# One attention-plus-mixer kernel: the mixer at six products a pair, and part of the output products moved between the row maxima

## The chip, the cores and the metric

The kernel runs on one core of a Trainium2 chip. The metric is the device time of one execution in microseconds (us); less is better.

## The reference

The input `x` has 2048 tokens of 512 channels. Two branches read its layernorm `xn`: a softmax attention with 32 heads of 16 channels, and the token-mixing block of MLP-Mixer, whose two matrices act along the tokens. The second branch gates the first.

```python
def _A_ref(x, wqkv, wo):                       # H = 32, Dh = 16
    qkv = (x @ wqkv).reshape(B, S, 3, H, Dh).transpose(2, 0, 3, 1, 4)
    q, k, v = qkv[0], qkv[1], qkv[2]
    p = softmax(einsum("bhqd,bhkd->bhqk", q, k) * Dh ** -0.5)
    o = einsum("bhqk,bhkd->bhqd", p, v)
    return o.transpose(0, 2, 1, 3).reshape(B, S, D) @ wo
def _B_ref(x, w1, b1, w2, b2):                 # F = 1792
    h = layernorm(x)
    u = gelu(einsum("bsd,sf->bdf", h, w1) + b1)
    return (einsum("bdf,fs->bds", u, w2) + b2).transpose(0, 2, 1)
xn = layernorm(x)
out = x + _A_ref(xn, A_wqkv, A_wo) * silu(_B_ref(xn, B_w1, B_b1, B_w2, B_b2))
```

All data are float32. Where the kernel multiplies matrices of the mixer or the output, each factor is held as an upper and a lower part in TensorE's one-pass format, and three products (upper by upper, upper by lower, lower by upper) are added.

## The kernel before, in words

**Stages.** A first stage of some 150 us makes q, k and v and stores them in DRAM. Then one hand-written loop over `s` (0 to 532 by two) does all the rest; one turn of it is called a *pair* here. Heads are worked two at a time: 16 head pairs `p`, each with two *spans* of 1024 queries and 16 blocks of keys. In one pair TensorE (PE) makes

- eight *maxima products* (`max_of`, L386) of queries by keys, 512 columns each, of which VectorE (DVE) takes row maxima (L390), while `s` is below `NU` = 512;
- eight *scores* (`score`, L724) with the maximum already subtracted through two extra rows of the operands; ScalarE (ACT) exponentiates them (L729) into `prob`;
- two times the *values* (`values`, L740): four 32-column products of `prob` by v and ones, summed over the 16 key blocks in the bank `av`.

Scores run 20 steps (`LEAD`) behind the maxima, so the loop has three parts: ten pairs with maxima alone, 246 *steady pairs* (`s` = 20 to 510) with both, and a *tail* of ten pairs (`s` = 512 to 530) with scores and values but without maxima. A closing stretch behind it finishes the last head pair (`own`, `one`, `two`, `chunk`) and writes the last eight row blocks.

**The filler.** All other work of PE is a list of *products* of 512 columns that a generator `everything()` gives out (`mixer()`, then `rest()`). In a steady pair `halves` takes up to six of them, cuts each into two pieces of 64 rows (L864), and `ORDERS` lays the pieces (D) between maxima (m) and scores (s) of the two heads:

```python
    2: ("smsmDDsmsm", "msmsmsmsDD", 3),
    4: ("sDDDDmsmsmsm", "msmsmsmDDDDs", 6),
    6: ("DDDDDDsmsmsmsm", "msmsmsmsDDDDDD", 7),
```

The first word is that of one head, the second that of the other, read position by position; at the number the values come in. How many are taken is set by `wanted(s)`, a straight line from the products done at the start to `n_fill` = 1344 at the pair `T_MIX`. Outside the steady pairs `whole` makes a product in one piece of 128 rows (L839).

**The mixer** has 14 blocks of 48 products (layer 1) and 16 blocks of 42 (layer 2), 1344 in all. A block sums in the only bank of `ps_dn` (`dn`). Behind a block's last product ACT reads the bank: `gelu` (L461) or `silu` (L494, L495); the next block's first product has to wait for that read. `ended` notes that a block has ended in a pair, and the next pair then takes at most two products. Layer 2 needs the results `u` of layer 1, which go through DRAM (`u_d`) and come back into the tiles `ub`.

**Division and output.** The sums of the heads (numerators and denominators) lie in DRAM by group `g` of eight heads (`ND` = 4 groups) and span. `divide` loads them, multiplies by the reciprocals, and writes upper and lower parts `oc` into free tiles of the pool `hu`; in steady pairs GpSimd (POOL) multiplies and subtracts, later DVE (`eng`). The output of a row block of 128 tokens is 12 products (four groups by three, `rest`), summed in `dn`; `finish` multiplies it by the gate on DVE (L700), adds `x` (L701), stores it if it is one of the last eight (L703), and loads `x` (L694) and the gate (L696) of the block after next into tiles with two buffers each. Row blocks 8 to 15 come first (their last two heads are added in the closing stretch), then 0 to 7 with the last two heads moved into the group-3 tile by four GpSimd DMAs (`move_in`). All of these 192 products lie in the tail.

**Queues.** All other DMAs are issued by SyncE (SP), in written order; one that waits holds up those behind it. ACT, DVE and POOL too work in written order.

Of the kernel before, what the change touches and what calls it, by code (L numbers as in the profile page):

```python
# [21 lines left out]
def tile_attention_token_mixer(ctx, tc, x, wqkv, wo, w1, b1, w2, b2, out):  # L22
    nc = tc.nc
    P = 128
# [32 lines left out]
    v_d = dram.tile([NB, P, NP * 48], F32, name="v_d")  # L57
    u_d = [dram.tile([P, 2, D], F32R, name=f"u_d{i}") for i in range(NF)]
    g_d = dram.tile([NB, P, D], F32, name="g_d")
    num_d = [[dram.tile([640, 512], F32, name=f"num_d{g}_{h}") for h in range(QH)] for g in range(ND)]  # L60
    rec_d = [[dram.tile([8, 1024], F32, name=f"rec_d{g}_{h}") for h in range(QH)] for g in range(ND)]

# [86 lines left out]

    with (  # L150
# [269 lines left out]
    def mixer():  # L420
        n = 0
        ub = []
        for i in range(NF + NB):
            nk = NB if i < NF else NF
            before = i < min(N_BEFORE, NF)
            if before and i % 2:
                ps = ps_av.tile([P, 512], F32, name="av")[:, :D]
            else:
                ps = ps_dn.tile([P, 512], F32, name="dn")[:, :D]
            for kb in range(nk):  # L430
                if kb % 4 == 0 and n:
                    w_load(n + 4)
                    w_split(n + 2)
                mv = hb[kb] if i < NF else ub[kb]
                for j, (w, m) in enumerate(((whs, 0), (whs, 1), (wls, 0))):
                    yield (
                        ps, lambda r, w=w[n], kb=kb: w[r, kb % 4, :], lambda r, mv=mv, m=m: mv[r, m, :],
                        kb == 0 and j == 0, kb == nk - 1 and j == 2,
                    )
                if kb % 4 == 3 or kb == nk - 1:  # L440
                    n += 1
                if i == NF - 1 and kb < NF - 1:
                    while kb not in stored:
                        yield None
                    ub.append(hu.tile([P, 2, D], F32R, name="hu"))
                    move(ub[kb], u_d[kb])
            yield (lambda i=i, ps=ps: gelu(i, ps)) if i < NF else (lambda i=i, ps=ps: silu(i - NF, ps))
            if i + 1 >= min(N_BEFORE, NF):
                yield None
            if i == NF - 1:  # L450
                while NF - 1 not in stored:
                    yield None
# [96 lines left out]
    multiplied = [0]  # L549
    HOMES = [("u", "sq")] * 3 + [("gt", "gt"), ("xt", "xt")] + [("u", "sq")] * (QH * ND - 5)  # L550

    def eng():

# [2 lines left out]
    def divide(m, g, span):  # L556
# [4 lines left out]
        num = [el.tile([P, 512], F32, name=nm) for nm in HOMES[m]]  # L561
        for c in range(2):
            nc.sync.dma_start(
                num[c][rows, :],
# [7 lines left out]
        def times():  # L572
            for c in range(2):
                eng().tensor_tensor(out=num[c][rows, :], in0=num[c][rows, :], in1=rec[rows, c, :], op=OP.mult)
            multiplied[0] += 1
            after(2, parts)


# [14 lines left out]
    def divisions():  # L593

        for x in list(undivided):
            if x == (2, 0) and now[0] < NU:
                break
            if x in away and begun_divisions[0] - len(divided) < 4 and begun_divisions[0] - multiplied[0] < 2:
                undivided.remove(x)
                divide(begun_divisions[0], *x)  # L600
                begun_divisions[0] += 1
                break
# [69 lines left out]
            sub(nc.vector, w[:, 1, :], raw, w[:, 0, :])  # L672


    xts = {}
    gts = {}
    held = []
    blocks = list(range(NB // 2, NB)) + list(range(NB // 2))

    def load_x_second(b):  # L680

        i = b - NB // 2
        if i % 4 == 0:
            held.append(big.tile([P, S], F32, name="big"))
        xts[b] = held[-1][:, i % 4 * 512 : i % 4 * 512 + 512]
        nc.sync.dma_start(xts[b], xv[:, b, :])

    def load_out(n):
        if n >= NB:
            return  # L690
        b = blocks[n]
        if n >= NB // 2:
            xts[b] = el.tile([P, D], F32, name="xt")
            nc.sync.dma_start(xts[b], xv[:, b, :])  # L694
        gts[b] = el.tile([P, D], F32, name="gt")
        nc.sync.dma_start(gts[b], g_d[b])  # L696

    def finish(n, ps):
        b = blocks[n]
        nc.vector.tensor_tensor(out=gts[b], in0=ps, in1=gts[b], op=OP.mult)  # L700
        nc.vector.tensor_tensor(out=xts[b], in0=xts[b], in1=gts[b], op=OP.add)  # L701
        if n >= NB // 2:
            nc.sync.dma_start(out[b * P : (b + 1) * P, :], xts[b])  # L703
        load_out(n + 2)

    gates = {}
# [41 lines left out]
    def rest():  # L748

        for n in range(N_W - 2, N_W):  # L750
            w_split(n)
        for n in range(2):
            load_out(n)
        load_last_w()

        def until(ready):
            while not ready():
                yield None

        yield from until(lambda: now[0] >= NU and all((g, QH - 1) in divided for g in range(ND)))  # L760
        for n, b in enumerate(blocks):
            if n == NB // 2:
                yield from until(lambda: own_done[0] and len(divided) == QH * ND)
            ps = ps_dn.tile([P, 512], F32, name="dn")[:, :D]
            at = slice(b % 4 * P, (b % 4 + 1) * P)
            for g in range(ND):
                o = oc[g, b // 4]
                rows = slice(0, DH * heads_of(g) if n < NB // 2 else P)
                for j, (m, w) in enumerate(((0, whs), (0, wls), (1, whs))):
                    w = w[N_MIX + g].rearrange("p a b -> p (a b)")  # L770
                    yield (
                        ps, lambda r, o=o, m=m, at=at, rows=rows: o[rows, m, at],
                        lambda r, w=w, rows=rows: w[rows, :],
                        g == 0 and j == 0, g == ND - 1 and j == 2,
                    )
            yield lambda n=n, ps=ps: finish(n, ps)
            yield None

# [92 lines left out]
    def wanted(s):  # L871
# [25 lines left out]
    for s in range(0, total + 1, 2):  # L897
        t = s - LEAD
        now[0] = s
        run_later()  # L900
        if s >= NU - 40:
            divisions()
        if 0 <= s - (NU - 12) < NB:
            load_x_second(NB // 2 + (s - (NU - 12)) // 2)
        heads = [items(s, a) for a in range(2)]
        if s < NU and t >= 0:
            steady[0] = True
            late = ended[0]
            n = max(0, min(6, round((wanted(s + 1) - done) / 2) * 2))
            one, two, then = halves(lead, min(n, 2) if late else n)  # L910
            made = [dict(D=part, m=heads[a][0], s=heads[a][1]) for part, a in ((one, lead), (two, 1 - lead))]
            first, second, middle = ORDERS[(len(one) + 1) // 2 * 2]
            if one:
# [32 lines left out]
        else:  # L946
            made = [heads[a][1] for a in range(2)]
            n = len(made[0])
            for i in range(n):
                made[1][i]()  # L950
                made[0][i]()
                if i == n - 2:
# [3 lines left out]
                    elif asides:  # L956
                        asides.pop(0)()
                    values(t - 2)
                    if (s - NU) // 2 % 2:
                        take(3 * ND, whole)  # L960
                    now[0] = s + 1
                    run_later()
            if 0 <= t - 1 < NT and (t - 1, 0, 0) in prob:
                if n:
                    values(t - 1)
                if s == total - 2:
                    load_gates(NB // 2, NB - 2)
                take(3 * ND, whole)
            if s == total - 6:
                split_last_w()  # L970
        if turn:
# [15 lines left out]
    load_gates(NB - 2, NB)  # L987
    run_later()
    one, two, chunk = asides
    take(4, whole)  # L990
    one(ps_sc, "sc")
    take(4, whole)
    ps = two()
    of = ks[NP - 1][:, :1024].rearrange("p (a q) -> p a q", a=2)
    left = []
# [1 line left out]
        chunk(ps, of, slice(k * P, (k + 1) * P))  # L997
    while open_ or later:
        run_later()
        take(3 * ND, lambda x, f: left.append(f) if f else whole(x, f))  # L1000
# [11 lines left out]

    for eng, some in ((nc.gpsimd, half[:4]), (nc.vector, half[4:])):
        for b in some:
            eng.tensor_tensor(out=gates[b], in0=xts[b], in1=gates[b], op=OP.add)
            nc.sync.dma_start(out[b * P : (b + 1) * P, :], gates[b])


# [25 lines left out]
```

## Time and profile before

| | us |
|---|---|
| three runs | 1710.68, 1712.19, 1715.19; median 1712.19 |
| the profiled execution: its own time | 1712.47 |
| the profiled execution: its span | 1710.7 |
| PE busy in the span | 1675.3 (98%) |
| DVE busy | 1414.7 (83%) |
| ACT busy | 1183.7 (69%) |
| POOL busy | 529.5 (31%) |

Times in the profile count from the start of the span. An instruction's line shows its start, its length, engine, line of the kernel, what it writes and reads, and in brackets how long the engine had been idle before and what ended that. Matmuls are pipelined: their lengths overlap, so distances between starts tell more than lengths. In a view by windows the columns are the window, its length, then for PE, weight loads, DVE, ACT and POOL the busy time and (x) the instructions, then the granted TensorE clock as a share of full speed, the DMA engines' busy share, and GB/s.

### The profile page before, as it was taken

The numbers are of one execution on the slowest core, as the hardware profiler recorded it, in microseconds if no ns is written. First come the engines' busy times: TensorE is split into PE (matmuls) and PEld (weight loads), VectorE is DVE, ScalarE is ACT, GpSimd is POOL, SyncE is SP. The second block draws the span as 40 slices with busy tenths as digits, with TensorE's granted clock in tenths as the row PEclk, the third lists the DMA queues.
The fourth block names the chain that finished last, engine by engine and source line by source line (L and its number), as shares of the span: only waits on it lengthen the run. The fifth ranks groups of instructions, "written<-read, shape, count | busy, mean of one in ns | idle before, by whom it ended". The sixth has DMA issues, their size and how long they took to land.

```text
span 1710.7 us, 30333 instructions
## 1 busy us (share of the span) xinstructions
PE 1675.3 (98%) x11626; PEld 839.1 (49%) x11626; DVE 1414.7 (83%) x2388; ACT 1183.7 (69%) x2283; POOL 529.5 (31%) x641
## 2 busy tenths in 40 slices
PE   7999999999999999999999999999999999999997
PEld 6887644444444444444444444444444444444454
DVE  6565888889888988888988888888889888888634
ACT  3333277777777777777777777777777777777752
POOL 4223831432234323431322222222222221263401
PEclk9999999999999999999999999999999999999999
DMA  6467611414151415144513223041414150541425
GB/s 222 177 235 184 133 32 45 78 45 65 39 90 40 66 40 90 45 82 166 102 33 57 46 52 65 23 81 35 75 36 74 40 82 17 92 138 54 135 92 185
DMA packets 146557, 145.04 MB, mean 85 GB/s; under 512 B 50972, under 2 KB 109340, under 8 KB 143340
## 3 DMA queue, kind: packets, MB, share of 16 engines
q1 hardware_dynamic: 141868, 142.10, 34.9%
q0 software_dynamic: 4544, 1.01, 0.4%
q8 instruction: 91, 1.49, 0.4%
q14 instruction: 54, 0.44, 0.1%
HBM read 95.04 MB, written 46.91 MB: 83 GB/s over the span
## 4 chain that ended last, share of the span: by engine, by line
PE 88%; DVE 6%; ACT 3%; DMA 1%; POOL 1%; issue 1%; SPq 0%; DVEq 0%; ACTq 0%; POOLq 0%
PE av L740 27%; PE dn L864 20%; PE mx L386 15%; PE sc L724 12%; DVE mxp L390 5%; PE dn L839 4%; PE mx L299 2%; PE sc L299 2%; ACT prob L729 2%; PE av L839 1%; PE dn L299 1%; PE av L299 1%; PE mx L724 1%; DMA vp<-v_d 1%; PE mx L401 0%
## 5 line engine op out<-in xcount | busy, mean ns | idle before, releaser
L390 DVE TENSOR_REDUCE mxp<-mx 128x1 f32<-128x512 f32 x2008 | 1249.2, 683 | 174.4 <-PE mx L386 89.1
L729 ACT ACTIVATE prob<-sc 128x512 f32<-128x512 f32 x2008 | 1041.7, 603 | 326.6 <-PE sc L724 236.2
L386 PE MATMUL mx<-big 48*128 48x512 f32 x2008 | 826.6, 432 | 3.2
L724 PE MATMUL sc<-big 50*128 50x512 f32 x2008 | 773.5, 431 | 6.3 <-ACT prob L729 3.0
L740 PE MATMUL av<-prob,vp 128*32 128x512 f32 x4096 | 545.8, 605 | 0.5 <-ACT ev L510 0.5
L864 PE MATMUL dn<-hu,wh 64*128 64x512 f32 x1570 | 515.5, 401 | 0.0
L386 PEld LDWEIGHTS mx<-big 48*128 48x128 f32 x2008 | 360.7, 186 | 235.9 <-DVE mxp L390 221.0
L724 PEld LDWEIGHTS sc<-big 50*128 50x128 f32 x2008 | 353.1, 186 | 229.4 <-ACT prob L729 204.3
L864 PE MATMUL dn<-hu,wl 64*128 64x512 f32 x786 | 320.3, 407 | 0.0
L864 PEld LDWEIGHTS dn<-hu,wh 64*128 64x128 f32 x1570 | 281.0, 186 | 48.0 <-issue 22.6
L864 PEld LDWEIGHTS dn<-hu,wl 64*128 64x128 f32 x786 | 145.7, 185 | 106.9 <-issue 75.5
L144 POOL CAST wh<-raw 128x512 fp32r<-128x512 f32 x106 | 61.7, 583 | 332.3 <-PE sc L724 174.7
L75 POOL TENSOR_TENSOR wl<-raw,wh 128x512 fp32r<-128x512 f32 x122 | 147.9, 1215 | 38.7 <-ACT wh L146 24.4
L740 PEld LDWEIGHTS av<-prob,vp 128*32 128x32 f32 x4096 | 80.7, 108 | 147.1 <-issue 134.9
L405 POOL CAST m<-f 16x128 fp32r<-16x128 f32 x32 | 9.0, 282 | 284.8 <-DVE f L404 284.8
L462 POOL TENSOR_TENSOR sq<-u 128x512 f32<-128x512 f32 x14 | 14.6, 1042 | 204.6 <-ACT u L461 204.6
L79 POOL DMA_DIRECT2D big<-m x128 | 68.0, 538 | 1.3 <-issue 1.2
L700 DVE TENSOR_TENSOR gt<-dn,gt 128x512 f32<-128x512 f32 x16 | 11.1, 691 | 44.1 <-PE dn L839 44.1
L729 ACT ACTIVATE prob<-mx 128x512 f32<-128x512 f32 x40 | 24.5, 613 | 32.0 <-PE sc L724 21.4
L839 PE MATMUL dn<-wh,hu 128*128 128x512 f32 (+1 forms) x128 | 44.5, 407 | 1.4 <-DVE gt L700 0.8
L498 POOL TENSOR_SCALAR t<-t 128x512 f32<-128x512 f32 x16 | 24.4, 1524 | 62.6 <-ACT t L495 62.5
L75 POOL TENSOR_TENSOR hu<-hx,hu 128x512 fp32r<-128x512 f32 x16 | 20.4, 1293 | 53.4 <-ACT hu L242 53.4
(201 smaller groups left out, 1026.0 us busy)
## 6 DMA issues: line engine op xcount, KB each, us to landing
raw<-in_B_w_dram SPq DMA_DIRECT2D x104, 256.0 KB
big<-k_d SPq DMA_DIRECT2D x96, 128.0 KB
big<-q_d SPq DMA_DIRECT2D x96, 128.0 KB
q_d<-sg SPq DMA_DIRECT2D x16, 512.0 KB
k_d<-sg SPq DMA_DIRECT2D x16, 512.0 KB
num_d<-ev SPq DMA_DIRECT2D x30, 256.0 KB
u_d<-uo SPq DMA_DIRECT2D x14, 512.0 KB
hu<-u_d SPq DMA_DIRECT2D x14, 512.0 KB
```

The source lines that it names most:

```text
L75: eng.tensor_tensor(out=o, in0=a, in1=b.bitcast(F32), op=OP.subtract)
L79: queue.dma_start(dst.bitcast(F32), src.bitcast(F32))
L144: nc.gpsimd.tensor_copy(whs[n][:, :m, :], raws[n][:, :m, :])
L299: nc.tensor.matmul(ps, w[part][:, kd, m], xt[kd][:, z, :], start=w is wh and z == 0 and kd == 0, stop=w is wl and kd == ND - 1,)
L386: nc.tensor.matmul(ps, q[o : o + 48, r * P : (r + 1) * P], k[o : o + 48, c * 512 : (c + 1) * 512], start=True, stop=True,)
L390: nc.vector.tensor_reduce(mxp[u // 16][:, a, r % 8, c : c + 1], ps, axis=AX.X, op=OP.max)
L498: nc.gpsimd.tensor_scalar(t, t, 1.0, None, op0=OP.add)
L724: nc.tensor.matmul(ps, ks[p][o : o + 50, kb * P : (kb + 1) * P], qs[p][o : o + 50, at : at + 512], start=True, stop=True,)
L729: nc.scalar.activation(e, ps, AF.Exp, scale=scale)
L740: nc.tensor.matmul(av[32 * j : 32 * j + 32, :], vps[p][:, kb, 16 * a : 16 * a + 32], prob.pop((t, a, c)), start=kb == 0, stop=kb == NB - 1,)
L839: nc.tensor.matmul(ps, w(slice(0, P)), m(slice(0, P)), start=first, stop=last)
L864: made.append(lambda r=r, start=first and a == lead, stop=last and a != lead: nc.tensor.matmul(ps, w(r), m(r), start=start, stop=stop,))
```

## The change

- The line of `wanted` ends at `T_MIX` = `NU` - 70 = 442 in place of 512, and the pair after a block's end may take four products in place of two. Once the mixer is done, a pair may take six more.
- Layer 2's first block is begun while the last of the fourteen tiles of `u` is still on its way; that tile is loaded just ahead of the three products that read it.
- The divisions of groups 0 to 2 (both spans) are all made in steady pairs, on POOL; only group 3's second span is left for the tail.
- Ten row blocks (`PARTS`: 0 to 9) get their nine products of groups 0 to 2 in steady pairs. `part` copies each sum out of `dn` on ACT, POOL multiplies it by the gate and adds `x`, and the result `y` goes to DRAM (`y_d`).
- In the tail these ten blocks have the three products of group 3 left; `finish` adds `y` in place of `x`. The other six keep all twelve.
- The splits of the last two quarters of `wo` go from ACT and DVE to POOL.

```diff
@@ w_split
-        if steady[0] and n < N_W - 2:
+        if steady[0]:
...
-        sub(nc.gpsimd if n < N_W - 2 else nc.vector, wls[n][:, :m, :], raws[n][:, :m, :], whs[n][:, :m, :])
+        sub(nc.gpsimd, wls[n][:, :m, :], raws[n][:, :m, :], whs[n][:, :m, :])
@@ mixer
+                if i == NF and kb == NF - 1:
+                    while NF - 1 not in stored:
+                        yield None
+                    ub.append(hu.tile([P, 2, D], F32R, name="hu"))
+                    move(ub[NF - 1], u_d[NF - 1])
+                    yield None
+                    yield None
...
-            if i == NF - 1:
-                while NF - 1 not in stored:
-                    yield None
-                ub.append(hu.tile([P, 2, D], F32R, name="hu"))
-                move(ub[NF - 1], u_d[NF - 1])
                 yield None
@@ divide, divisions
-    undivided = [(g, span) for span in (1, 0) for g in range(ND)]
+    undivided = [(g, span) for span in range(QH) for g in range(ND - 1)]
+    undivided += [(ND - 1, span) for span in range(QH)]
...
-            if x == (2, 0) and now[0] < NU:
-                break
-            if x in away and begun_divisions[0] - len(divided) < 4 and begun_divisions[0] - multiplied[0] < 2:
+            if x in away and begun_divisions[0] - len(divided) < 2:
@@ new
+    def part(b, ps):
+        y = el.tile([P, D], F32, name="t")
+        nc.scalar.copy(y, ps)
+        def two():
+            nc.gpsimd.tensor_tensor(out=y, in0=y, in1=gts[b], op=OP.mult)
+            nc.gpsimd.tensor_tensor(out=y, in0=y, in1=xts[b], op=OP.add)
+            load_part(b + 2)
+            after(3, lambda: store_y(b, y))
+        after(2, two)
+    def store_y(b, y):
+        nc.sync.dma_start(y_d[b], y)
+        if b >= NB // 2:
+            unkept.append(b)
+    PARTS = NB // 2 + 2
+    unkept = list(range(PARTS, NB))
@@ load_out, finish
-            xts[b] = el.tile([P, D], F32, name="xt")
-            nc.sync.dma_start(xts[b], xv[:, b, :])
+            ys[b] = el.tile([P, D], F32, name="xt")
+            nc.sync.dma_start(ys[b], y_d[b])
...
-        nc.vector.tensor_tensor(out=xts[b], in0=xts[b], in1=gts[b], op=OP.add)
+        nc.vector.tensor_tensor(out=ys[b], in0=ys[b], in1=gts[b], op=OP.add)
@@ rest
+        for b in range(PARTS):
+            yield from until(lambda: all((g, b // (NB // QH)) in divided for g in range(ND - 1)))
+            ps = ps_dn.tile([P, 512], F32, name="dn")[:, :D]
+            yield from products(ps, b, range(ND - 1))
+            yield lambda b=b, ps=ps: part(b, ps)
+            yield None
+        load_last_w()
+        yield from until(lambda: now[0] >= NU and (ND - 1, QH - 1) in divided)
...
+            if b >= PARTS:
+                yield from products(ps, b, range(ND), rows)
+            else:
+                yield from products(ps, b, [ND - 1], rows)
@@ pace
-    T_MIX = total - LEAD
+    T_MIX = NU - 70
...
-        return start + share * (n_fill - start)
+        return start + share * (n_fill - start) + (6 if done == n_fill else 0) if share < 1 else done + 6
...
-        if s >= NU - 40:
+        if done >= n_fill // 2 + 3 * NF:
             divisions()
...
-            one, two, then = halves(lead, min(n, 2) if late else n)
+            one, two, then = halves(lead, min(n, 4) if late else n)
@@ tail
-                    if (s - NU) // 2 % 2:
-                        take(3 * ND, whole)
+                    take(3 * ND, whole)
```

More of the change, by code (lines that the diff above doesn't have):

```diff
@@ L560, in divide @@
         rec = el.tile([P, 2, 512], F32, name="uo")
-        num = [el.tile([P, 512], F32, name=nm) for nm in HOMES[m]]
+        num = [el.tile([P, 512], F32, name=nm) for nm in ("u", "sq")]
         for c in range(2):
@@ L751, in rest @@
             w_split(n)
-        for n in range(2):
-            load_out(n)
-        load_last_w()
+        for b in range(2):
+            load_part(b)
         def until(ready):
@@ L758, in until, with products @@
                 yield None
[L760 to L764, printed above, removed]
+        def products(ps, b, groups, rows=None):
             at = slice(b % 4 * P, (b % 4 + 1) * P)
-            for g in range(ND):
+            for g in groups:
                 o = oc[g, b // 4]
-                rows = slice(0, DH * heads_of(g) if n < NB // 2 else P)
+                at_g = rows if g == ND - 1 else None
                 for j, (m, w) in enumerate(((0, whs), (0, wls), (1, whs))):
@@ L965, in tile_attention_token_mixer @@
                     values(t - 1)
-                if s == total - 2:
-                    load_gates(NB // 2, NB - 2)
-                take(3 * ND, whole)
+                    if s == total - 2:
+                        load_gates(NB // 2, NB - 2)
+                    take(3 * ND, whole)
             if s == total - 6:
@@ L989, in tile_attention_token_mixer @@
     one, two, chunk = asides
-    take(4, whole)
     one(ps_sc, "sc")
-    take(4, whole)
+    take(3, whole)
     ps = two()
@@ L999, in tile_attention_token_mixer @@
         run_later()
-        take(3 * ND, lambda x, f: left.append(f) if f else whole(x, f))
+        take(3, lambda x, f: left.append(f) if f else whole(x, f))
     for f in left:
```

42 lines of the change are left out of this document (27 added, 15 removed).

## The prediction

> **What bounds the kernel now.** I read the page's busy times first, then its chain that ended last, and then went through the loop pair by pair with the view by windows.
>
> ```profile
> PE 1675.3 (98%) x11626; PEld 839.1 (49%) x11626; DVE 1414.7 (83%) x2388; ACT 1183.7 (69%) x2283; POOL 529.5 (31%) x641
> ...
> PE 88%; DVE 6%; ACT 3%; DMA 1%; POOL 1%; issue 1%; SPq 0%; DVEq 0%; ACTq 0%; POOLq 0%
> ```
>
> PE carries the chain. But what a filler product costs depends on where it lies, so I want the price of one in a steady pair and in the tail. DVE takes eight maxima in each steady pair, so I set the windows from the first maximum of one pair to the first of another: four pairs without filler, two with two products each, two with four, six with six; then one pair with six products and one with two in which also a span's maxima are turned; four pairs with six products in which ACT also copies quotients; and two pairs with two products that follow a `silu`.
>
> ```profile
> 806.73:827.54 20.81, 19.90 (x130) 7.01 (x130) 20.02 (x34) 16.89 (x33) 8.89 (x9) 1.00 0.23 76
> 350.39:360.91 10.52, 10.38 (x74) 4.11 (x72) 9.88 (x16) 8.88 (x18) 4.78 (x5) 1.00 0.17 51
> 1443.23:1454.19 10.96, 10.96 (x82) 4.66 (x78) 9.93 (x17) 8.91 (x18) 1.89 (x2) 1.00 0.00 1
> 833.53:868.01 34.48, 34.48 (x266) 16.59 (x264) 29.82 (x48) 26.15 (x51) 6.48 (x8) 1.00 0.56 85
> 827.54:833.53 5.99, 5.99 (x48) 2.85 (x46) 5.16 (x11) 4.13 (x8) 3.18 (x7) 1.00 0.02 5
> 1057.05:1062.94 5.89, 5.48 (x40) 2.12 (x38) 5.16 (x10) 4.43 (x9) 3.65 (x7) 1.00 0.02 4
> 1568.70:1593.08 24.38, 23.88 (x179) 11.05 (x177) 20.36 (x34) 20.78 (x41) 12.58 (x12) 1.00 0.31 95
> 913.69:919.52 5.83, 5.35 (x38) 2.21 (x38) 5.11 (x10) 4.42 (x9) 2.78 (x2) 1.00 0.46 141
> 1454.19:1460.11 5.92, 5.45 (x38) 2.21 (x38) 4.96 (x8) 4.53 (x10) 3.86 (x4) 1.00 0.32 101
> ```
>
> A pair takes 5.20 us with no product (20.81/4), 5.26 with two, 5.48 with four, 5.75 with six (34.48/6). DVE is busy 20.02 of 20.81 us without filler and 29.82 of 34.48 with six, PE the other way round: the pair begins as DVE's and ends as PE's. Two more products cost 0.06, 0.22 and 0.27 us, so a product costs 0.03 to 0.135 us there.
>
> The tail's windows: the whole of it (first score after the last maximum to the end of the last values), a pair with one block of twelve, a pair with two.
>
> ```profile
> 1603.75:1692.09 88.34, 85.90 (x465) 46.59 (x461) 34.12 (x54) 47.82 (x94) 11.13 (x18) 1.00 0.38 121
> 1652.43:1658.70 6.27, 6.27 (x37) 3.16 (x37) 1.41 (x3) 2.98 (x7) 0.00 (x0) 1.00 0.25 86
> 1658.70:1667.91 9.21, 9.21 (x49) 5.33 (x49) 2.73 (x4) 5.18 (x11) 0.00 (x0) 1.00 0.41 141
> 1670.83:1672.85 2.02, 2.02 (x17) 0.78 (x16) 1.90 (x3) 1.51 (x4) 0.00 (x0) 1.00 0.74 260
> ```
>
> A block of twelve costs 2.94 us (9.21 - 6.27), 0.245 a product, with PE busy throughout; a pair without one is 3.33. ACT, at 47.82 of 88.34 us, is not the bound. So a product moved from the tail into a steady pair is paid at about half.
>
> **The steady pairs.** From the written order of the two programs I counted the 246 pairs by their products. Before: 4 with none, 40 with two, 57 with four, 145 with six (1178 products). After: 3 with none, 25 with two, 1 with three, 38 with four, 11 with five, 168 with six (1268). At the prices above, three and five put halfway, that is 1376.9 before and 1387.9 after: **+11.0 us** for 90 more products.
>
> Thirty pairs also turn a span's maxima, which costs 0.24 us on six products (5.99) and 0.63 on two (5.89), 0.43 on four by the mean. Before, 18 of them have six, 6 four, 6 two; after 23, 4, 2 and one none: **-1.5**.
>
> Seven pairs of two products in layer 2 cost 5.82 to 5.94 in place of 5.26; the first and the last are the windows from 913.69 and 1454.19. Together 4.4 us. Six of the seven follow a pair of four, where `silu` stands in ACT's queue ahead of the pair's last exponential. After a pair that ends its block with two products, `silu` stands behind all exponentials:
>
> ```profile
> 1306.20 0.72 ACT L494 ACTIVATE ev<-dn,b2h 128x512 f32<-128x512 f32 x1
> 1306.60 0.50 PE L724 MATMUL sc<-big 50*128 50x512 f32 x1
> ...
> 1307.17 4.95 DVE L390 TENSOR_REDUCE mxp<-mx 128x1 f32<-128x512 f32 x8 [0.32 <-PE mx L386]
> ```
>
> and the eight maxima of the next pair run without a gap. In the changed order every mixer block ends in a pair of two or three, every row block in one of five with its pieces last: **-4.4**. But the next pair may now take four, and its first piece stands second in `ORDERS`, not fifth. In the rows above that place comes at 1306.94 (0.34 after the score) and ACT has read the bank at 1306.92, so I take 0.1 us for each of 37 block ends: **+4**. No row shows such a pair. The bounds: nothing, if the read is just in time, and 0.64 each (23.7 us) if it waits like the seven; the row is much nearer to the first.
>
> Quotients copied by ACT inside a pair of six cost 0.35 (24.38/4 = 6.10 against 5.75). Before, four divisions lay so, after seven: **+1.0**.
>
> `part` adds an ACT copy and two POOL operations in ten places:
>
> ```profile
> L510 ACT COPY ev<-av 128x512 f32<-128x512 f32 x32 | 18.8, 588 | 19.4 <-PE av L740 19.4
> ...
> L499 POOL TENSOR_TENSOR t<-t,ev 128x512 f32<-128x512 f32 x16 | 20.6, 1286 | 1.3
> ```
>
> The copy (0.59, shorter than the 0.72 of `silu`'s read) stands behind the exponentials and is priced with the block ends. POOL gets 26 us for the parts and some 16 for the added divisions, over 200 us in which it was under half busy; nobody waits for it within two pairs. If it did fall behind, PE would wait for the split weights: up to 1.3 us a time. The early begin of layer 2 replaces four pairs without filler by pairs of 5, 0 and 3 products, already counted; its tile is asked for two pairs (10 us) before use. SP gets 20 loads and 10 stores for the parts and 10 loads of `y`, fewer of `x`; each load is asked for two blocks (22 us) ahead, behind `load_qk` and `load_v`, which keep their places. Nothing.
>
> Steady pairs together: 11.0 - 1.5 - 4.4 + 4 + 1.0 = **+10.1**.
>
> **The tail.** Ten pairs at 3.33 and sixteen blocks at 2.94 make 80.3 of the 88.3 us; 8.0 go to other things. Of a block, the first product takes longer:
>
> ```profile
> 1652.36 0.50 PE L839 MATMUL dn<-wh,hu 128*128 128x512 f32 x1
> 1652.70 0.39 PE L839 MATMUL dn<-wl,hu 128*128 128x512 f32 x1
> 1652.93 0.63 PE L839 MATMUL dn<-wh,hu 128*128 128x512 f32 x2
> ```
>
> 0.34 to the second, then 0.23. A block of three is 0.34 + 2 x 0.236 = 0.81. The Trainium skill, TensorEngine Tiling (Array Packing), section Key Properties, says that changing the tiling mode drains the array; the trace agrees with 0.11 us more on the first product, and this speaks a little against the change, since cut blocks keep all sixteen such starts. Blocks after: 6 x 2.94 + 10 x 0.81 = 25.7 against 47.0, **-21.3**. The other things after:
>
> ```profile
> 1607.77 1.00 ACT hu L587 x2
> ...
> 1629.47 0.66 PE mx L617 x4
> ...
> 1639.60 1.16 PE mx L629 x8
> ```
>
> - First pair 1.5: its block of three needs the last quotient's lower part, which ACT (to 1608.77) and DVE behind it give at 1609.1, 5.4 after the tail's start; 5.6 in place of 4.1. The splits of `wo`, which held up the block before, are gone.
> - Transposes and broadcast of `own`: 0.66 + 1.16 = 1.8, as before.
> - Block 0 needs the four GpSimd DMAs of `move_in`:
>
> ```profile
> 1643.77 1.96 POOL L79 DMA_DIRECT2D hu<-uo x4 [26.38 <-issue]
> ...
> hu<-uo POOLq DMA_DIRECT2D x4, 64.0 KB, 2.3
> ```
>
> The third is issued by 1645.1 and lands 2.3 later, 7.4 to 7.8 after the broadcast began at 1639.60 (estimate). Only one block lies between now, so PE is there after 6.5: 0.9 or a little more.
> - Blocks 0 to 7 come two a pair, three products each, and the pair would take 3.33 + 1.6 = 4.95. Their loads may not keep up:
>
> ```profile
> 1667.98 0.34 SPq L703 DMA_DIRECT2D out_dram<-xt  x1
> 1670.00 0.33 SPq L694 DMA_DIRECT2D xt<-in_A_x_dram  x1
> 1670.39 0.43 SPq L696 DMA_DIRECT2D gt<-g_d  x1
> ...
> 1677.20 0.69 DVE L700 TENSOR_TENSOR gt<-dn,gt 128x512 f32<-128x512 f32 x1 [3.66 <-PE dn L839]
> ```
>
> A store is issued at 1667.98, the tile's next load at 1670.00, and the DMA window above ends at 1672.85: 4.9 us, and with two DVE operations of 0.7, 6.4 from a block's end to the end of the block after next. Three such hops behind block 0, less the slack of 1.9 us until PE needs the bank, put PE some 3.3 us behind.
> - The last pairs have no products, so the last values wait for eight exponentials, one each 0.48 us:
>
> ```profile
> 1639.92 0.60 ACT L729 ACTIVATE prob<-mx 128x512 f32<-128x512 f32 x1
> 1640.40 0.62 ACT L729 ACTIVATE prob<-sc 128x512 f32<-128x512 f32 x1
> ```
>
> 5.6 from first score to last value in place of 3.33: 2.3.
>
> Together 9.8 against 8.0, and the tail is 33.3 + 25.7 + 9.8 = 68.8: **-19.5**. The closing stretch (18.6 us to the span's end) keeps its work.
>
> **Sum.** 1712.5 (the profiled execution, 0.3 above the median of the runs) + 10.1 - 19.5 = **1703**.
>
> **The rivals.**
>
> *Each block end stops PE (slower).* The place: the second position of the pair behind a block's end, with `dn`'s only bank still unread and ACT held by `silu`. For it: the seven pairs above lost 0.64 so, and now every such pair takes four products and has no slack on DVE. Against: 1306.92 against 1306.94. At 0.64 for each of 37 ends, 23.7 in place of 4: 1723. It decides against the change from 0.49 an end. Chance 0.10.
>
> *The tail is bound by its loads and ACT.* If stores and loads of successive blocks, all on SP's queue, delay one another, the hop is nearer 8 us than 6.4 and block 0's wait 2: some 6 us more, 1709. For it: SP waits in order. Against: DMA share 0.74 for only 2 of 6 us. Chance 0.15.
>
> *The tail's waits slow the clock.*
>
> ```profile
> 204.83:206.88 2.05, 0.00 (x1) 0.03 (x2) 0.00 (x0) 0.00 (x0) 2.04 (x5) 1.00 0.04 6
> 209.50:216.50 7.00, 7.00 (x34) 4.02 (x33) 6.20 (x10) 5.42 (x10) 6.69 (x7) 0.51 0.52 123
> ```
>
> PE stood still for 2.05 us, and soon after the granted clock was 0.51 for 7 us. In the tail one such fall takes up to 3.5 us of PE's work; two make 1710. The waits I count are 0.9 to 1.5 us each. The Trainium skill, TensorE: Matmul & The Clock Gate, section HAM oscillation — how this bites in real kernels, sets the limit at idle gaps above about 3.4 us; this trace differs, with 2.05. Chance 0.05.
>
> *More is gained.* Block ends cost nothing and the loads keep up: 4 + 3.3 less, 1696. Chance 0.10.
>
> **How the numbers follow.** The forecast keeps 0.60. The range 1695 to 1713 takes in the bounds below, the loads and the clock, and leaves out the first rival and a little beside it. About 0.3% (5 us) is what a measurement of this kernel tells from no change. Under 1707: nearly all of the forecast and of the larger gain, a third of the loads' and the clock's cases, 0.75. Within 0.3%: 0.15. Slower: 0.10.
>
> **What would show it.** Right: pairs of six at 5.75 us throughout, pairs of four behind a block's end under 5.7, a tail of about 69 us, blocks 0 to 6 some 6.4 us apart by twos. Wrong: idle time of PE before L909 (the pieces) that ACT or POOL ends; pairs of the late stretch above 6 us; a tail above 76 us; a clock under 1.00 in it.

## The result, and the profile after

The changed kernel takes **1715.17 us** (median of 14 runs, 1713.22 to 1718.69) against 1712.55 for the kernel before (14 runs beside it). The ratio is **1.0017**, with a 95% interval of 1.0009 to 1.0025: slower by 0.17%, which by the prediction's own bound of 0.3% is no change. 1703 was forecast, and 1715.17 lies above the range. The profiled execution of the changed kernel took 1717.66 us, 2.5 more than the median; the second profile of this kernel, below, suggests where this surplus lies.

The page's busy times and the first line of its chain, after:

```profile
PE 1675.4 (98%) x11716; PEld 847.0 (49%) x11716; DVE 1410.0 (82%) x2378; ACT 1188.3 (69%) x2291; POOL 566.9 (33%) x673
...
PE 88%; DVE 5%; DMA 2%; ACT 2%; POOL 1%; issue 1%; SPq 0%; DVEq 0%; POOLq 0%; ACTq 0%
```

PE is busy for as long as before (1675.3), and the span is 4.8 us longer (1715.5 against 1710.7), so PE is idle for longer; besides, work at a lowered clock counts as busy. Where the time lies is seen from the starts of the maxima, pair by pair. From the first steady pair to the last, the loop takes 1411.2 us in place of 1391.4: +19.8. Two pairs alone hold 9.8 of that. The view by windows shows them first, then the tail in two parts and as a whole, then four pairs of six products and a pair of four behind a block's end:

```profile
1483.03:1492.60 9.57, 6.87 (x38) 2.45 (x36) 5.04 (x8) 6.45 (x13) 9.41 (x10) 0.86 0.59 135
1515.50:1526.48 10.98, 8.13 (x42) 3.90 (x44) 5.16 (x9) 5.05 (x9) 2.54 (x2) 0.69 0.61 193
1621.57:1661.85 40.28, 38.61 (x213) 20.42 (x212) 15.17 (x26) 22.47 (x44) 4.75 (x10) 1.00 0.26 74
1661.85:1696.39 34.54, 28.75 (x160) 10.14 (x160) 12.27 (x18) 21.47 (x42) 0.00 (x0) 0.90 0.51 161
1621.57:1696.39 74.82, 67.36 (x372) 30.55 (x371) 27.43 (x44) 43.93 (x86) 4.75 (x10) 0.95 0.37 114
1270.30:1293.30 23.00, 23.00 (x178) 11.07 (x176) 20.52 (x34) 16.52 (x32) 3.80 (x4) 1.00 0.07 20
1304.57:1310.25 5.68, 5.68 (x42) 2.97 (x44) 5.06 (x8) 4.86 (x10) 3.85 (x4) 1.00 1.01 118
```

A pair of six still takes 5.75 (23.00/4), and PE fills it. The pair of two products at 1483.03 takes 9.57 where such pairs take 5.27; the pair of four at 1515.50 takes 10.98 for 5.48. In both POOL, ACT or a transfer holds PE, and the clock falls. The tail takes 74.82 in place of 88.34, but 68.8 was forecast. Its first 40.28 us hold 1.7 us of idle PE (1.6 in the fastest kernel below). The last 34.54, in which eight row blocks have three products each, hold 5.8 us of idle PE and a clock of 0.90.

**The pair at 1483.03.** POOL's timeline, then ACT's, then PE's, of the changed kernel:

```profile
1479.68 0.28 POOL L406 CAST m<-f 16x128 fp32r<-16x128 f32 x1 [8.46 <-DVE f L405]
...
1480.44 2.12 POOL L80 DMA_DIRECT2D big<-m  x4
1482.58 1.30 POOL L76 TENSOR_TENSOR hu<-u,hu 128x512 fp32r<-128x512 f32 x1
...
1485.07 1.27 POOL L575 TENSOR_TENSOR u<-u,uo 128x512 f32<-128x512 f32 x1
1486.30 1.26 POOL L575 TENSOR_TENSOR sq<-sq,uo 128x512 f32<-128x512 f32 x1
```

```profile
1486.37 0.62 ACT L587 CAST hu<-u 128x512 fp32r<-128x512 f32 x1 [1.81 <-POOL u L575]
1487.59 0.62 ACT L587 CAST hu<-sq 128x512 fp32r<-128x512 f32 x1 [0.60 <-POOL sq L575]
```

```profile
1488.76 0.99 PE L755 MATMUL sc<-big 50*128 50x512 f32 x2 [2.63 <-ACT prob L760]
```

POOL stood idle for 8.46 us, because in its written order the turn of a span's maxima came next and its input was not there. Then it did the turn, the turn's four DMAs, the subtractions of one division and the multiplications of the next in one burst. ACT's copies of the quotients stand in ACT's order ahead of exponentials; they waited for those multiplications, and the scores waited for the exponentials. POOL is busy for 33% of the span, and still PE stands still for 2.63 us.

**The pair at 1515.50.** SP's waits (us in total, times, longest) from 1460 to 1530, then SP's timeline, then one row of ACT's and one of PE's:

```profile
SPq L564 <- POOL hu L76: 20.9, 3, 16.8
SPq L80 <- DMA uo<-rec_d: 6.9, 1, 6.9
```

```profile
1489.78 0.33 SPq L80 DMA_DIRECT2D big<-k_d  x1
...
1507.45 0.30 SPq L80 DMA_DIRECT2D big<-q_d  x1
...
1509.58 5.04 SPq L522 DMA_DIRECT2D d<-ev  x2
...
1515.16 0.38 SPq L502 DMA_DIRECT2D g_d<-t  x1
```

```profile
1517.71 0.58 ACT L692 COPY t<-dn 128x512 f32<-128x512 f32 x1 [3.03 <-DMA g_d<-t]
...
1518.35 0.79 PE L909 MATMUL dn<-wh,hu 64*128 64x512 f32 x1 [2.92 <-ACT t L692]
```

SP waited 16.8 us for POOL to free the numerators' tiles (L564), so seven loads went out directly ahead of `load_qk` (L80), whose twelve transfers then took from 1489.78 to 1507.75. Behind them, and behind the transfers of a span's sums that waited 4.2 us for ACT (L522), stands the store of `silu`'s last gate (L502), issued at 1515.16. The tile of that store is named `t`, with two buffers, and `part` takes its `y` from the same name: the ACT copy of a prepared block had to wait until the gate had landed in DRAM. The copy reads the bank `dn`, so the next block's first product waited for it, and PE stood still for 2.92 us.

**The tail.** The rows of SP and of DVE in the last eight blocks:

```profile
1664.27 0.34 SPq L734 DMA_DIRECT2D out_dram<-xt  x1
...
1671.39 0.38 SPq L734 DMA_DIRECT2D out_dram<-xt  x1
1674.88 0.32 SPq L725 DMA_DIRECT2D xt<-y_d  x1
1675.25 0.42 SPq L727 DMA_DIRECT2D gt<-g_d  x1
1675.77 0.38 SPq L734 DMA_DIRECT2D out_dram<-xt  x1
...
1680.17 0.38 SPq L734 DMA_DIRECT2D out_dram<-xt  x1
...
1688.70 6.31 SPq L734 DMA_DIRECT2D out_dram<-xt  x2
```

```profile
1678.66 0.69 DVE L731 TENSOR_TENSOR gt<-dn,gt 128x512 f32<-128x512 f32 x1 [2.94 <-DMA gt<-g_d]
1679.39 0.69 DVE L732 TENSOR_TENSOR xt<-xt,gt 128x512 f32<-128x512 f32 x1
```

One buffer's round goes from the store at 1671.39 to the store at 1680.17: 8.78 us for two blocks. It consists of the store (3.5 until its tile may be loaded again), two issues (0.8), the gate's landing (3.0, to 1678.66) and DVE (1.5). The prediction had 6.4. The store at 1675.77 belongs to the other buffer. The rounds of this buffer before and after it, 1664.27 to 1671.39 and 1680.17 to 1688.70 (the last row stands for two stores, of which this is the first), took 7.12 and 8.53 us.

### The profile page after: what moved, and what is told of

Same layout as the page of the kernel before. It is cut to its first block, busy times and chain, and to the rows that moved or that the text cites. A ratio compares the mean times of both kernels' runs of the same rounds, so it can differ in the third digit from the quotient of the medians.

```text
span 1715.5 us, 30670 instructions
## 1 busy us (share of the span) xinstructions
PE 1675.4 (98%) x11716; PEld 847.0 (49%) x11716; DVE 1410.0 (82%) x2378; ACT 1188.3 (69%) x2291; POOL 566.9 (33%) x673
## 4 chain that ended last, share of the span: by engine, by line
PE 88%; DVE 5%; DMA 2%; ACT 2%; POOL 1%; issue 1%; SPq 0%; DVEq 0%; POOLq 0%; ACTq 0%
PE av L771 27%; PE dn L909 26%; PE mx L387 12%; PE sc L755 11%; DVE mxp L391 4%; PE mx L300 2%; PE sc L300 2%; PE dn L884 2%; ACT prob L760 1%; DMA out_dram<-xt 1%; PE av L300 1%; PE dn L300 1%; DMA raw<-in_B_w_dram 1%; PE mx L755 0%; PE mx L402 0%
## 5 line engine op out<-in xcount | busy, mean ns | idle before, releaser
L909 PE MATMUL dn<-hu,wh 64*128 64x512 f32 x1570 | 572.5, 405 | 0.0
L387 PEld LDWEIGHTS mx<-big 48*128 48x128 f32 x2008 | 364.4, 186 | 221.1 <-DVE mxp L391 206.0
L909 PEld LDWEIGHTS dn<-hu,wh 64*128 64x128 f32 x1570 | 288.5, 185 | 172.2 <-issue 145.6
L909 PE MATMUL dn<-hu,wl 64*128 64x512 f32 x786 | 316.1, 402 | 0.0
L909 PEld LDWEIGHTS dn<-hu,wl 64*128 64x128 f32 x786 | 145.5, 185 | 8.2 <-issue 0.8
L80 POOL DMA_DIRECT2D big<-m x128 | 67.7, 535 | 0.0
L909 PE MATMUL dn<-wh,hu 64*128 64x512 f32 x120 | 42.9, 411 | 2.9 <-ACT t L692 2.9
```

Source lines behind the costliest of these rows:

```text
L80: queue.dma_start(dst.bitcast(F32), src.bitcast(F32))
L387: nc.tensor.matmul(ps, q[o : o + 48, r * P : (r + 1) * P], k[o : o + 48, c * 512 : (c + 1) * 512], start=True, stop=True,)
L909: made.append(lambda r=r, start=first and a == lead, stop=last and a != lead: nc.tensor.matmul(ps, w(r), m(r), start=start, stop=stop,))
```

## The experiments

Each kernel was run beside the kernel before on one chip. The ratios are to that kernel; the changed kernel's is 1.0017.

**Own tile for y.**

```diff
-        y = el.tile([P, D], F32, name="t")
+        y = el.tile([P, D], F32, name="y")
```

> The changed kernel, with one edit: the row blocks' prepared sum y has a tile name of its own instead of the two buffers named t that it shares with silu. Theory (the ACT copy of the third prepared block stood behind a buffer whose store was late on SP's queue): the pair from 1515.50, 10.97 us long, falls to about 5.5, the granted clock there is back at 1.00, and the time is 5.5 us under the changed kernel, about 1709.7. Rival (SP's queue is what is late, and the copy's successors on POOL need loads from the same queue, so the wait only moves to the next product or to POOL): within 1 us of the changed kernel, about 1715.

1713.89 us, ratio 1.0005 (0.9996 to 1.0013). The two pairs in its profile:

```profile
1483.99:1494.09 10.10, 7.41 (x38) 2.79 (x36) 5.04 (x9) 6.49 (x13) 9.94 (x10) 0.73 0.69 164
...
1517.24:1522.72 5.48, 5.48 (x43) 2.45 (x42) 4.97 (x9) 4.10 (x8) 2.31 (x2) 1.00 0.57 189
```

The second pair is at 5.48 with a clock of 1.00, as the theory has it. The time fell by some 2 us (0.0012 in the ratio, and the intervals overlap) and not by 5.5.

**Quotient copies later.** A pair has two halves; `after(n, f)` has `f` done n halves later.

```diff
-            after(2, parts)
+            after(4 if done < n_fill else 2, parts)
```

> The changed kernel, with one edit: the ACT copies of a division's quotients come four half pairs after its multiplications instead of two, for the divisions that end before the mixer does. Theory (ACT stood in its order behind POOL, which did a turn, its four DMAs and two divisions in one burst): the pair from 1483.03, 9.58 us long, falls to about 5.3, the clock there is 1.00, and the time is 4.3 us under the changed kernel, about 1710.9. Rival (the tiles come free a pair later, SP's loads are still later, and what is won is lost at the pair from 1515.50): 1715 or more, with that pair at 11 us or longer.

1719.72 us, ratio 1.0038 (1.0026 to 1.0051): the rival's side. The two pairs, and ACT's copy in the second:

```profile
1483.79:1489.62 5.83, 5.75 (x37) 2.00 (x34) 5.04 (x9) 5.80 (x12) 5.75 (x6) 1.00 0.09 16
...
1512.87:1529.29 16.42, 7.62 (x42) 3.41 (x44) 5.16 (x8) 4.94 (x9) 2.56 (x2) 0.69 0.69 160
```

```profile
1521.03 0.59 ACT L692 COPY t<-dn 128x512 f32<-128x512 f32 x1 [8.97 <-DMA g_d<-t]
```

The first pair is cured, 5.83 for 9.57, with a clock of 1.00: that ACT's copies waited for POOL's burst behind the turn was its cause. The tiles come free later and SP's loads go out later with them (1487.23 against 1483.90 for the first), and at the shared tile that becomes a wait of 8.97 us: more is lost there than was won here.

**Own buffers for the last eight blocks.** Blocks 10 to 15 of the tail's order get other tiles for y and gate: two use `u` and `sq`, four use tiles of `hu`. They are loaded while the whole blocks run.

```diff
+        if n >= NB - 4:
+            both = hu.tile([P, 2, D], F32R, name="hu").bitcast(F32)
+            ys[b], gts[b] = both[:, 0, :], both[:, 1, :]
...
-        load_out(n + 2)
+        if n < NB // 2:
+            load_out(n + 2)
+        for k in {4: (10, 11), 5: (12, 13), 7: (14, 15)}.get(n, ()):
+            load_out(k)
```

> The changed kernel, with one edit: each of the last eight row blocks has buffers of its own for y and gate (tiles that are free by then), loaded before the block's turn, so that no load waits for a store. Theory (in the changed kernel a store, the next load and the next store follow one another on SP's queue, 4.3 us a block): the 6.4 us in which PE stands still behind block 0 go, the clock in the tail is back at 1.00 (2.9 us more), the tail is about 66 to 67 us and the time about 1706. Rival (ACT's eight exponentials a pair and the two divided pairs set the pace, not the loads): the tail keeps most of its 75.6 us, and the time is 1711 to 1715.

1707.23 us, ratio 0.9968 (0.9958 to 0.9979), 0.49% under the changed kernel's, 8.4 us. From the start of the last steady pair to the end it takes 89.97 us in place of 98.67, and the clock in the tail is at 1.00. (The 75.6 us of the expectation counts the tail's 74.82 and the 0.8 behind the last values.) ACT was not the bound. In this profile the pair of the shared tile took 6.59 us, not 10.98, though the order up to there is the same.

**The three edits together.**

> The changed kernel with the three edits together (own tile for y, quotient copies later, own buffers for the last eight blocks). Theory (three separate causes): the gains add, 5.5 + 4.3 + 9.3 = 19 us under the changed kernel, about 1696, so 16 us under the kernel before. Rival (the two long pairs have one common cause, SP's lateness, and one edit cures or moves both): 1700 to 1705.

1701.03 us, ratio 0.9932 (0.9919 to 0.9944): 14.5 us under the changed kernel. By the time this lies with the rival, by the profile not: both long pairs are gone, each by its own edit (5.83 and 5.48), and the sum of 19 was too large because it took 5.5 us for the second from one profile. A pair of 6.82 is left, in which ACT waits 0.94 us for a buffer of `y`. Singly measured gains do not add here: the later copies alone make the wait at the shared tile longer, so they are worth something only when that wait is taken away too.

**The gate ahead of y.** Both keep two buffers.

```diff
+        gts[b] = el.tile([P, D], F32, name="gt")
+        nc.sync.dma_start(gts[b], g_d[b])
         if n >= NB // 2:
             ys[b] = el.tile([P, D], F32, name="xt")
             nc.sync.dma_start(ys[b], y_d[b])
-        gts[b] = el.tile([P, D], F32, name="gt")
-        nc.sync.dma_start(gts[b], g_d[b])
```

> The changed kernel, with one edit: a block's gate is asked for before its y (the gate's tile is free when DVE has done the block two before, y's only when that block's store has landed). Theory (each of the two buffers goes round in 8.7 us: store 3.5, two issues 0.8, the gate's landing 3.0, two DVE operations 1.4, and the gate's share of it need not wait for the store): the round falls to about 7.3, three rounds give 4.2 us, with the clock's part 4 to 5, so about 1710.5. Rival (what makes the store slow, 3.5 us against 2.0 in the kernel before, is the loads in front of it in the same queue, and the gate now stands in front of it too): the store takes longer by what is won, within 1 us of the changed kernel, 1715.

1708.05 us, ratio 0.9978 (0.9969 to 0.9987). SP's rows of one round, and the tail's last part:

```profile
1664.36 0.38 SPq L734 DMA_DIRECT2D out_dram<-xt  x1
...
1667.51 0.32 SPq L727 DMA_DIRECT2D xt<-y_d  x1
...
1671.51 0.38 SPq L734 DMA_DIRECT2D out_dram<-xt  x1
```

```profile
1658.60:1687.80 29.20, 26.24 (x160) 9.44 (x160) 12.19 (x18) 21.36 (x42) 0.00 (x0) 1.00 0.66 202
```

The round is 7.15 us, 7.3 expected, and the clock stays at 1.00. From the store to the tile's next load it is 3.15 us, no longer than the 3.5 of before, so the rival falls. From the start of the last steady pair to the end it takes 92.84 us, 5.8 less than in the changed kernel; 4 to 5 were expected.

**Without the prepared blocks.**

```diff
-    PARTS = NB // 2 + 2
+    PARTS = 0
...
-            nc.sync.dma_start(ys[b], y_d[b])
+            nc.sync.dma_start(ys[b], xv[:, b, :])
```

> The changed kernel without its prepared row blocks: all sixteen are done whole in the tail, as in the kernel before; the mixer at six products a pair, the order of the divisions and the early layer 2 stay. Theory (the 90 products moved do cost about half in the steady pairs): the 21 pairs from 1492.60 fall from 124.3 us to about 110 (8.8 for the products, 5.5 for the long pair), the tail rises to about 88, so 1713 to 1714; the long pair from 1483.03 stays at 9 to 10 us, since no prepared block has begun by then. Rival (the loads of the prepared blocks are what holds SP and with it the division): that pair falls to 5.3 too, 1709.

1715.05 us, ratio 1.0023 (1.0014 to 1.0032). The long pair, the 21 pairs behind it, and the tail:

```profile
1483.55:1493.39 9.84, 7.12 (x38) 2.49 (x36) 5.05 (x9) 6.49 (x13) 9.68 (x10) 0.83 0.56 131
1493.39:1604.24 110.85, 105.05 (x676) 36.69 (x674) 105.30 (x174) 90.09 (x176) 22.50 (x29) 1.00 0.29 57
1607.46:1694.48 87.02, 86.40 (x471) 47.14 (x471) 28.96 (x46) 45.41 (x89) 5.90 (x11) 1.00 0.35 112
```

All three as the theory has them; the time is 1 us above it. So the long pair does not come from the prepared blocks; with the second experiment, it is the divisions' work on POOL, which this kernel keeps.

**Three buffers for the divisions.** `gelu`, which uses tiles of the same two names, is given the three buffers too.

```diff
-        num = [el.tile([P, 512], F32, name=nm) for nm in ("u", "sq")]
+        num = [el.tile([P, 512], F32, name=nm, bufs=3) for nm in ("u", "sq")]
...
-            if x in away and begun_divisions[0] - len(divided) < 2:
+            if x in away and begun_divisions[0] - len(divided) < 3:
```

> The changed kernel, with one edit: three buffers instead of two for each of the two tiles that a division's numerators go to, and up to three divisions under way, so that SP's loads for the next division do not wait 16.8 us for POOL. Theory (the long pair at 1515.50 comes from SP's lateness, which begins there): the queue is free some 15 us earlier, the pair falls from 7 to 11 us to about 5.5 with y still sharing its buffers with silu; the pair at 1483.03 keeps 8 us or more, since POOL's burst behind the turn is the same; 1710 to 1712. Rival (load_qk, twelve transfers that each wait for a reader, sets when the queue is free): the pair at 1515.50 stays, 1714 to 1715.

1713.51 us, ratio 1.0012 (1.0003 to 1.0021). SP's rows, and the two pairs:

```profile
1490.72 0.33 SPq L80 DMA_DIRECT2D big<-k_d  x1
...
1497.14 0.30 SPq L80 DMA_DIRECT2D big<-q_d  x1
...
1505.81 0.41 SPq L502 DMA_DIRECT2D g_d<-t  x1
```

```profile
1483.67:1493.48 9.81, 7.11 (x38) 2.49 (x36) 5.03 (x8) 6.49 (x13) 9.65 (x10) 0.83 0.23 40
...
1515.94:1521.41 5.47, 5.47 (x42) 2.43 (x42) 4.97 (x8) 4.09 (x8) 2.32 (x2) 1.00 0.34 106
```

The gate is stored 9.4 us earlier, and the second pair is at 5.47 with `y` still in the shared tile. So both were needed for its wait, SP's lateness and the shared tile. The time lies between the theory's and the rival's. My picture of the lateness was wrong in part: `load_qk` does not begin earlier than in the changed kernel (1490.72 against 1489.78). It is through in 6.7 us and not in 18. In the changed kernel it waited 12.2 us in all for the landings of the seven loads directly ahead of it (6.9, 2.4, 2.3 and 0.6). With three buffers SP issues nothing between 1469.84 and `load_qk`, and in this stretch it waits for no such landing. The part from the last steady pair to the end took 100.31 us here against 98.67. Its last part took 36.43 us in place of 34.54, with the same 5.8 us of idle PE and a clock of 0.86 in place of 0.90.

**A third buffer for y**, on top of the three edits.

```diff
-        y = el.tile([P, D], F32, name="y")
+        y = el.tile([P, D], F32, name="y", bufs=3)
```

> The kernel with the three edits together (1701), and a third buffer for the prepared sum y. Theory (the pair from 1523.6 in that run, 6.83 us, waits 0.94 us in ACT's queue for y's buffer, whose store is late on SP): it falls to 5.86, 1700. Rival (the next product waits for its loads instead): no change, 1701.

1700.45 us, ratio **0.9934** (0.9922 to 0.9947): faster than both kernels. The pair of 6.82 is at 5.86; in the time this cannot be told from the kernel of the three edits. Its 21 late pairs, and its tail in two parts and as a whole:

```profile
1489.74:1608.78 119.04, 118.53 (x856) 54.64 (x858) 105.86 (x174) 96.47 (x189) 52.25 (x53) 1.00 0.50 127
1613.48:1653.74 40.26, 38.67 (x211) 20.40 (x212) 15.19 (x26) 22.47 (x44) 4.76 (x10) 1.00 0.43 131
1653.74:1679.79 26.05, 26.02 (x160) 9.47 (x160) 12.28 (x18) 21.14 (x42) 0.00 (x0) 1.00 0.52 176
1613.48:1679.79 66.31, 64.69 (x371) 29.87 (x371) 27.46 (x44) 43.61 (x86) 4.76 (x10) 1.00 0.47 149
```

The tail's last part falls from 34.54 to 26.05 and is full; the first part is unchanged (40.28, 40.26).

**The changed kernel again.**

> The changed kernel once more, unaltered, for a second profile of the pair that was 10.97 us long and a comparison on one chip with the next kernel. Theory (that pair's wait is a race between SP's queue and ACT, so its size varies from execution to execution: with the same program up to there it was 6.59 and 6.14 us in two other profiles): 5.5 to 11 us there, 9.5 to 10.1 for the pair of the POOL burst, the tail within 1 us of 75.6, the time about 1715. Rival (it is fixed by the order, and the other two profiles differ by their tails' other placement): 10.9 us again.

1714.56 us, ratio 1.0016 (1.0007 to 1.0025). The pair of the shared tile takes 9.42 us here. In four profiles with the same order up to there it took 10.98, 9.42, 6.59 and 6.15, so its length varies from execution to execution. Both profiled executions of the changed kernel are among its longest (1717.66 and 1717.36, 2.5 and 2.8 above the median), while the two with the short pair lie within 0.8 us of their kernel's median. So the ordinary run probably pays less for this pair than the two profiles show. The small gain of the first experiment agrees with that; a profile of an ordinary run of the changed kernel is missing.

**The three causes cured otherwise.** The diffs of the later copies, of the gate ahead of y and of the three division buffers, and no other; `y` is in the shared tile.

> The changed kernel with the three causes taken away in other ways than in the kernel of 1700.5: y still shares its two buffers with silu, but the divisions have three buffers and up to three under way (SP's queue on time); the quotient copies come four half pairs after the multiplications; and the last blocks keep two buffers, the gate asked for ahead of y. Theory (three causes, each cured by whatever takes away its own wait): no pair of the late stretch above 6.2 us, tail as with the gate first (about 5.8 us less than the changed kernel), 1702 to 1704. Rival (own buffers themselves were the cure): the pair at 1515.50 is long again, 1707 or more.

1702.43 us, ratio 0.9942 (0.9928 to 0.9955), as the theory has it; no steady pair from 1484 on is above 5.94. The cures can be exchanged, so it is the waits that cost the time, not some one tile.

## Why the prediction was wrong

The profiled spans differ by +4.8: the steady loop begins 1.8 us earlier, takes 10.0 more in its ordinary pairs and 9.8 more in two long ones, and what follows it takes 13.2 less. Of the prediction's own signs of being wrong, three appeared: idle PE ended by ACT before a piece (L909), late pairs above 6 us, and a clock under 1.00 in the tail. A tail above 76 us did not.

**Right: the price of the products.** The steady pairs without the two long ones cost +10.0; +10.1 was forecast. A pair of six stayed at 5.75. The terms were not all exact: 24 pairs of four behind a block's end took 5.67 by the mean, 0.19 above the plain 5.48 and not 0.1, so those ends cost some 2 us more, and smaller differences took that back: that the sum agrees to 0.1 is partly luck. The kernel without the prepared blocks and the fastest one agree: 90 products cost 8.2 us between the maxima (119.04 less 110.85), 0.09 each, and 20.7 in the tail (87.02 less 66.31), 0.23 each.

**Wrong: "Nothing" for POOL.** The step was that nobody waits for POOL within two pairs, since it is under half busy. The divisions now fall into pairs in which POOL stands in its order behind a turn, and ACT's copies follow the multiplications by one pair. That cost 4.3 us in the profile after, and the later copies took 3.7 of it away (9.57 to 5.83). I had written down the price (up to 1.3 us a time) for another case, split weights that come late.

**Wrong: "Nothing" for SP and for the ACT copy.** The step was that each load is asked for 22 us ahead, behind `load_qk` and `load_v`. I followed the loads' due times but not the stores that stand behind them, nor the names of the tiles. The fewer division buffers (two kinds of tile where there had been four) delayed SP, and `part` takes a tile that such a store still reads. That cost 5.5 us in the profile after, and probably less in an ordinary run. Either cure takes it away.

**Mis-sized: the tail's loads.** The 6.4 us of a round were read from one store in the kernel before that took 2.0 us until the next load, and from loads taken as landed when the DMA engines fell idle 2.0 us after the second was issued. That trace also has a store that took 2.98 us (1678.64 to 1681.62), and DVE waited for PE there, so no row showed when a load had really landed. Here the two terms were 3.5 and 3.0, and the three rounds behind block 0 took 7.12, 8.78 and 8.53. The forecast gave 3.3 us for these waits and no fall of the clock. Idle PE and the clock together cost 8.5 us in the last part (34.54 less 26.05). The three rounds are 24.4 us in place of 19.2, and these 5.2 more are what the 8.5 exceed the 3.3 by. Without the idle PE and the low clock the tail is 66.31, near the 65.5 (68.8 less 3.3) that the other terms give. The second rival, 1709 with loads and stores that delay one another, described this mechanism. I held against it that the DMA share was 0.74 for only 2 of 6 us; that share did not show the chain of latencies.

**The other rivals.** A block's end cost 0.19 us and not 0.64. The clock did fall, in the two long pairs and in the tail; with the waits gone it stays at 1.00 there, so it is their consequence. The mixer at six products a pair and the new order of the divisions, without the prepared blocks, would be near nothing: that kernel stands 3.9 us above the kernel before, with 4.6 in its long pair. What the moved products bring, 12.5 us (20.7 less 8.2), was real and was lost to the three waits; with them gone the kernel came to 1700.45, against a forecast of 1703 with 3.3 us of waits in it.

## What to carry to other kernels

A half idle engine that works in written order can still be late at one place: look at what stands ahead of each added instruction, and at what that waits for. Two uses of one tile name can become a wait, as long as the queue that touches the tile is late (3.03 us here, 8.97 with the later copies, none with SP on time), so list for each moved step the buffers it shares, with the last reader of each. For a load behind a store, add up the whole round of one buffer (store, issue, landing, use) under the traffic of the new kernel, and take from it every transfer that need not wait.

## What the runs showed of the hardware

The clock, in windows of 1.2 us in and behind the idle time that ended at 1488.76 and of 1.5 us in the tail of the changed kernel:

```profile
1486.80:1488.00 1.20, 0.00 (x0) 0.00 (x0) 0.58 (x1) 0.60 (x2) 1.20 (x2) 1.00 0.41 125
...
1490.40:1491.60 1.20, 1.20 (x8) 0.00 (x0) 0.31 (x1) 1.17 (x3) 1.12 (x2) 0.50 1.05 195
```

```profile
1682.00:1683.50 1.50, 0.31 (x4) 0.00 (x0) 0.58 (x1) 0.94 (x2) 0.00 (x0) 0.50 0.55 212
```

After 2.63 us without work PE ran at half speed from about 1490 to 1493. The Trainium skill, TensorE: Matmul & The Clock Gate, section HAM oscillation — how this bites in real kernels, speaks of idle gaps above some 3.4 us; here 2.63 was enough. In the tail no single gap behind block 0 was above 1.99 us, and after three of them (0.91, 1.99, 1.50) the clock was at a half from about 1681 to 1688. The Trainium skill, TensorE: Matmul & The Clock Gate, section A second HAM failure mode: psum-queue depth-cycling, tells of short idle times of PE between groups of matmuls, frequent enough to make the clock fall and rise; the trace agrees in that a fall followed several short gaps. Gaps of 0.61 to 1.21 us in the kernel with the gate first left it at 1.00.

SP waited 6.9 us in `load_qk` for the landing of a division's reciprocals, of which `load_qk` reads nothing. Whether that is room in the queue was not tried.
